# k transposed by DMA through bit planes from the ninth block on, its product with the decay on GpSimd, v loaded once

## The chip, the cores and the metric

One core of a Trainium2 chip runs the whole program. The metric is device microseconds of one execution, given as the median of the runs. The engines are called PE (matrix multiply), PEld (its weight loads), DVE (vector), ACT (scalar), POOL (GpSimd) and SP (here only a queue that issues DMAs).

## The reference

Three layers follow one another. The first is a linear attention with a state per head, the second a feed-forward layer with g = h·cos(h), the third a soft mixture of experts over all 3072 tokens.

```python
batch, n_heads, seq, head_dim = (4, 8, 768, 48)
for t in range(S):
    kt, vt, rt, wt = (k[:, :, t], v[:, :, t], r[:, :, t], w[:, :, t])
    cur = np.einsum('bhd,bhe->bhde', u[None] * kt, vt)
    y[:, :, t] = np.einsum('bhd,bhde->bhe', rt, state + cur)
    state = wt[:, :, :, None] * state + np.einsum('bhd,bhe->bhde', kt, vt)
...
h = x @ w_in
g = h * np.cos(h)
x = g @ w_out
...
logits = x @ phi                      # softmax over tokens fills slots, softmax over slots mixes them back
slot_out[e] = np.maximum(slot_input[e] @ w1[e], 0.0) @ w2[e]
```

All tensors are float32.

## The kernel before

The 3072 tokens go through in 24 blocks of 128 (six blocks per batch item; block j reads 128 steps of all eight heads). Blocks are numbered from 0. Inside a block the recurrence is cut into two chunks of 64 steps, c = 0 and 1.

For block j the attention steps are: `lw`, `lk`, `lr`, `lv`, `lz` load w, k, r, v (`lz` loads v a second time, with rows and heads placed so that it can stand beside the state in `rzs`, the stationary operand of the output). `wT`, `rT`, `kT` transpose w, r and k on PE, four 128x128 transposes each into one PSUM bank (`transpose4`, the call is line 145). `scan` and `sp` are two running products of the decay on DVE (L160 and L168). `ks` multiplies the transposed k with the decay on DVE (L195), `kN` transposes that back on PE (L213), `ksn` copies it to SBUF, `A` is the attention inside a chunk (L206), `U` the sum of k times v (L257). `z` (POOL from block 5 on, L267) decays the state, `st` adds U to it (DVE, L278), `rz` copies it into `rzs` (ACT), `y` is the output of the block (PE, L289). `ru`, `bo`, `bs` and `D` make the term with u: two products on POOL (L173, L174), a sum on DVE, two small copies on ACT, and a diagonal written by POOL (L220).

The feed-forward layer works on pieces h.t.q: block t, q one of four groups of 512 hidden columns. `h` is nine matmuls (L443 to L445), then `turns` (ACT), `rest` (DVE), `cos` (ACT), `mul` (DVE) make g. Of each block's four pieces three are transposed by DMA in blocks 3 to 19: `gz` copies the 32-bit values on ACT into two planes of 16 bits (L492), `gd` writes the planes to DRAM (L497), `gx` reads them back with a DMA transpose (L501). The rest is transposed on PE (`gT`) and copied (`gc`). `l` multiplies with phi folded into w_out (L510). `sum` to `es` are the running softmax over tokens. After the last block a fixed part computes the experts and the output (lines 722 to 891); the weights of the experts are loaded by `att`, `we` and `late0`.

The order of everything up to there is written out in the string `HEAD`: one word per step, and each engine, and the queue of SP, carries out its instructions in the order of that list. A DMA on SP waits in the queue for what it reads, and everything behind it waits with it. The first third of the list also decodes the weights of the feed-forward layer on ACT and DVE. The PSUM pool `ps_a` has three banks, which `wT`, `rT`, `kT`, `kN`, `A`, `U` and `y` take in turn.

Of the kernel before, what the change touches and what calls it, by code (L numbers as in the profile page):

```python
# [22 lines left out]
def rwkv_moe_kernel(ctx: ExitStack, tc: tile.TileContext, r, k, v, w, u, w_in, w_out, phi, w1, w2, cst, out):  # L23
    nc = tc.nc
# [255 lines left out]
    def e_y(j):  # L280

        L, rz = lt[j % 2], rzs[j % 2]
# [781 lines left out]
```

## Time and profile before

| | us |
|---|---|
| median of 3 runs | 482.76 (482.46 to 484.51) |
| the profiled execution, whole | 482.29 |
| its span | 480.5 |
| PE busy | 452.2 (94%) |
| DVE busy | 403.0 (84%) |
| ACT busy | 356.0 (74%) |
| POOL busy | 122.3 (25%) |

The span runs from the first to the last instruction of the trace; 1.8 us of the profiled execution lie around it. Matmuls overlap each other in the trace, so a busy PE says only that one was under way; the step from one start to the next is what it really takes.

### The profile page before, as it was taken

The numbers are of one execution on the slowest core, as the hardware profiler recorded it, in microseconds if no ns is written. First come the engines' busy times: TensorE is split into PE (matmuls) and PEld (weight loads), VectorE is DVE, ScalarE is ACT, GpSimd is POOL, SyncE is SP. The second block draws the span as 40 slices with busy tenths as digits, with TensorE's granted clock in tenths as the row PEclk, the third lists the DMA queues.
The fourth block names the chain that finished last, engine by engine and source line by source line (L and its number), as shares of the span: only waits on it lengthen the run. The fifth ranks groups of instructions, "written<-read, shape, count | busy, mean of one in ns | idle before, by whom it ended". The sixth has DMA issues, their size and how long they took to land.

```text
span 480.5 us, 15374 instructions
## 1 busy us (share of the span) xinstructions
PE 452.2 (94%) x6313; PEld 345.6 (72%) x6313; DVE 403.0 (84%) x783; ACT 356.0 (74%) x727; POOL 122.3 (25%) x162
## 2 busy tenths in 40 slices
PE   1889899999999999999999999999999999988993
PEld 1567688887877878767778678687787777755573
DVE  3999999998998999999999999899998986665242
ACT  5799989877788788877877787778888655573242
POOL 2421231423433223023325121513323000002110
PEclk9999999999999999999999999999999999999997
DMA  9998999343795984799679979977769879699938
GB/s 214 309 297 211 171 211 208 59 74 84 139 199 127 162 173 139 153 193 172 140 158 158 204 157 177 188 120 149 179 135 130 233 256 411 247 337 405 368 125 272
DMA packets 205589, 94.21 MB, mean 196 GB/s; under 512 B 181840, under 2 KB 187216, under 8 KB 205520
## 3 DMA queue, kind: packets, MB, share of 16 engines
q1 hardware_dynamic: 205520, 93.23, 81.1%
q8 instruction: 50, 0.82, 0.7%
q14 instruction: 19, 0.16, 0.1%
HBM read 61.75 MB, written 18.09 MB: 166 GB/s over the span
## 4 chain that ended last, share of the span: by engine, by line
PE 74%; DVE 11%; ACT 5%; DMA 4%; SPq 3%; issue 1%; POOL 0%; ACTq 0%; POOLq 0%
PE h L443 12%; PE h L445 11%; PE h L444 11%; PE l L510 5%; PE E L606 4%; PE y L289 4%; PE gT L478 4%; PE A L206 3%; PE U L257 3%; PE hps L797 2%; PE so L834 2%; PE wT L145 2%; PE kT L145 2%; DVE g L462 2%; PE rT L145 2%; PE kN L213 2%
## 5 line engine op out<-in xcount | busy, mean ns | idle before, releaser
L443 PE MATMUL h<-wu,x 128*128 128x512 f32 x288 | 121.9, 423 | 0.2
L445 PE MATMUL h<-wu,x 128*128 128x512 f32 x288 | 113.2, 393 | 0.0
L444 PE MATMUL h<-wu,x 128*128 128x512 f32 x288 | 112.6, 391 | 0.0
L466 ACT ACTIVATE g<-g,half_pi 128x512 f32<-128x512 f32 (+1 forms) x97 | 69.5, 720 | 17.0 <-DVE g L462 16.0
L458 ACT ACTIVATE g<-h 128x512 int32<-128x512 f32 (+1 forms) x96 | 57.1, 595 | 32.9 <-PE h L445 25.0
L471 DVE TENSOR_TENSOR g<-g,h 128x512 f32<-128x512 f32 x96 | 64.7, 676 | 9.0 <-ACT g L466 8.1
L462 DVE SCALAR_TENSOR_TENSOR g<-g,h 128x512 f32<-128x512 int32 (+1 forms) x96 | 64.7, 675 | 8.6 <-ACT g L458 7.7
L443 PEld LDWEIGHTS h<-wu,x 128*128 128x128 f32 x288 | 54.3, 189 | 18.2 <-DVE g L471 2.3
L445 PEld LDWEIGHTS h<-wu,x 128*128 128x128 f32 x288 | 54.0, 188 | 12.3
L444 PEld LDWEIGHTS h<-wu,x 128*128 128x128 f32 x288 | 54.4, 189 | 8.7
L220 POOL TENSOR_SCALAR_AFFINE_SELECT lt<-bo 64x512 f32<-64x512 f32 x48 | 38.0, 793 | 68.1 <-ACT bo L248 57.7
L492 ACT COPY zg<-g 128x1024 uint16<-128x1024 uint16 x51 | 52.8, 1042 | 1.8 <-DVE g L471 1.2
L267 POOL TENSOR_TENSOR z<-st_state,qt 128x192 f32<-128x192 f32 x35 | 22.0, 629 | 118.3 <-DVE st_state L278 94.2
L173 POOL TENSOR_TENSOR ru<-rn,u_b 128x384 f32<-128x384 f32 x24 | 26.1, 1086 | 81.5 <-DVE bo L243 32.1
L275 ACT COPY rzs<-z 64x192 f32<-64x192 f32 x96 | 33.4, 348 | 1.4 <-DVE z L263 0.4
L232 DVE COPY_PREDICATED lt<-cs,A 64x256 f32<-64x256 uint32 x72 | 32.2, 447 | 1.9 <-PE A L206 0.4
L189 DVE TENSOR_TENSOR lt<-rT,pt 64x512 f32<-64x512 f32 x48 | 32.8, 684 | 0.8 <-PE rT L145 0.3
L168 DVE TENSOR_TENSOR_SCAN pt<-wf,ini_f 128x520 f32<-128x520 f32 x24 | 30.9, 1289 | 0.0
L160 DVE TENSOR_TENSOR_SCAN qt<-wf,one_b 128x520 f32<-128x520 f32 x24 | 29.8, 1242 | 0.0
L289 PEld LDWEIGHTS y<-lt,rzs 128*32 128x32 f32 x1536 | 23.5, 110 | 6.2 <-issue 3.7
L174 POOL TENSOR_TENSOR ru<-ru,kn 128x384 f32<-128x384 f32 x24 | 26.9, 1120 | 2.0 <-DMA kn<-in_k_dram 0.2
L478 PE MATMUL gT<-cs,g 128*128 128x128 f32 x180 | 27.1, 275 | 0.0
(175 smaller groups left out, 808.7 us busy)
## 6 DMA issues: line engine op xcount, KB each, us to landing
we<-in_moe_w_dram SPq DMA_DIRECT2D x16, 1536.0 KB, 9.3
gs<-zg SPq DMA_DIRECT2D x51, 256.0 KB, 2.5
rawo<-in_moe_w_out_dram SPq DMA_DIRECT2D x8, 768.0 KB, 5.1
wn<-in_w_dram SPq DMA_DIRECT2D x24, 192.0 KB, 4.6
kn<-in_k_dram SPq DMA_DIRECT2D x24, 192.0 KB, 4.3
rn<-in_r_dram SPq DMA_DIRECT2D x24, 192.0 KB, 4.5
vn<-in_v_dram SPq DMA_DIRECT2D x24, 192.0 KB, 4.2
rzs<-in_v_dram SPq DMA_DIRECT2D x96, 48.0 KB, 3.1
```

The lines of the kernel that those rows point to most:

```text
L220: nc.gpsimd.affine_select(out=lt[j % 2][h, a], in_=bo_t[j][h, a].unsqueeze(2).to_broadcast([64, NS, C]), pattern=[[0, NS], [-1, C]], compa ...
L275: nc.scalar.copy(rzs[j % 2][64 * a:64 * a + 64, c, :, a, RZ[a]], z_t[j, c][64 * a:64 * a + 64])
L289: nc.tensor.matmul(ps[m:m + 32, o, c * C:(c + 1) * C], lhsT=rz[:, c, p, a, 32 * b:32 * b + 32], rhs=L[:, a, 2 * p + c, :], start=m not in ...
L443: nc.tensor.matmul(half[:, f], lhsT=xh[:, c, :], rhs=wh, start=(c == 0), stop=False)
L444: nc.tensor.matmul(half[:, f], lhsT=xl[:, c, :], rhs=wh, start=False, stop=False)
L445: nc.tensor.matmul(half[:, f], lhsT=xh[:, c, :], rhs=wl, start=False, stop=(c == KD - 1))
L458: nc.scalar.activation(gt.bitcast(I32), hp, AF.Copy, bias=0.25, scale=1.0 / TWO_PI)
L462: nc.vector.scalar_tensor_tensor(out=gt, in0=gt.bitcast(I32), scalar=-TWO_PI, in1=hp, op0=ALU.mult, op1=ALU.add)
L466: nc.scalar.activation(gt, gt, AF.Sin, bias=half_pi[:, 0:1])
L471: (nc.gpsimd if pool else nc.vector).tensor_tensor(out=gt, in0=gt, in1=hp, op=ALU.mult)
L478: nc.tensor.transpose(ps[:, m * 128:(m + 1) * 128], gt[:, m * 128:(m + 1) * 128], ident)
L492: copy(zg, g_t[t, q].bitcast(U16).rearrange("p (f i) -> p i f", i=2))
```

## The change

From block 8 on (`JK`) the step `kT` is gone. In its place `kz` copies the loaded k on POOL into two planes of 16 bits, `kd` writes them to DRAM and `kx` reads them back with a DMA transpose, in the manner and with the buffers of `gz`, `gd` and `gx` (which get one more `gx` buffer). `ks` then reads SBUF and not PSUM, and runs on POOL. `lv` is gone for all 24 blocks: `vc` copies on POOL half of what `U` needs from the tile that `lz` has loaded, and `U` reads the other half straight from there; `rzs` gets a third buffer. The tile `pts` moves to another pool. The list `HEAD` is a new one, with the same steps otherwise.

```diff
+    JK = range(8, 24)
+    NRZ = 3
-    NGS = 51
+    NGS = 67
-    NGX = 4
+    NGX = 5
-    vn = [nat.tile([128, H, D], F32, name=f"vn{i}") for i in range(2)]
+    vn = [nat.tile([128, HP, D], F32, name=f"vn{i}") for i in range(2)]
-    rzs = [nat.tile([128, 2, HP, 2, 64], F32, name=f"rzs{i}") for i in range(2)]
+    rzs = [nat.tile([128, 2, HP, 2, 64], F32, name=f"rzs{i}") for i in range(NRZ)]
+    def copy_v(j):
+        for c in range(2):
+            nc.gpsimd.tensor_copy(vn[j % 2][64 * c:64 * c + 64], rzs[j % NRZ][64 - 64 * c:128 - 64 * c, c, :, c, RZ[c]])
-        nc.vector.tensor_tensor(out=ks, in0=ps, in1=segs(qt, 2, C), op=ALU.mult)
+        (nc.gpsimd if j in JK else nc.vector).tensor_tensor(out=ks, in0=ps, in1=segs(qt, 2, C), op=ALU.mult)
-  ... rhs=vn[j % 2][h, 2 * p + a], start=True, stop=True)
+  ... rhs=vn[j % 2][h, p] if a == c else rzs[j % NRZ][h, c, p, a, RZ[a]], start=True, stop=True)
-        wt_t["p", u_] = aw.tile([128, 128], F32, tag="pts", name=f"pts{u_}", bufs=1)
+        wt_t["p", u_] = sm_p.tile([128, G], F32, tag="lg", name=f"pts{u_}", bufs=1)[:, 0:128]
+    def e_kz(j):
+        zg = xb_p[0].tile([128, 2, 512], U16, tag="zg", name=f"zk{j}", bufs=NZG)
+        nc.gpsimd.tensor_copy(zg, kn[j % 2].rearrange("p h d -> p (h d)").bitcast(U16).rearrange("p (f i) -> p i f", i=2))
+        zg_t["k", j] = zg
+    def e_kd(j):
+        b_gd("k", j)
+    def e_kx(j):
+        b_gx("k", j)
+        pend["kT", j] = gt_t.pop(("k", j))
...
-raw.i.1 raw.i.0 q.i.1 lw.0 abs.i.1 cs lk.0 q.i.0 lr.0 ... lv.0 rT.0 wf.0 d2b.i.0
```

What the new list does to the engines is shown at three places near the end of the attention. In the names a number is a running count of tiles; `kn_122` holds k of an odd block, `ks` the product, `gx` and `gxk` transposed pieces.

PE, before, from the transpose of k of block 23 (`kT`) to its `kN`, with the two pieces of h between them cut to their first row:

```order
L510 MATMUL l_6000<-gx_1_5975,p_sb 32x128 x4
L145 MATMUL kT_6013<-cs,kn_122 128x128 x4
L443 MATMUL h_1_6024<-wu_322,x_116 128x512
...
L145 MATMUL rT_6034<-cs,rn_120 128x128 x4
L443 MATMUL h_2_6041<-wu_468,x_116 128x512
...
L510 MATMUL l_6000<-gx_2_6039,p_sb 32x128 x4
L510 MATMUL l_6000<-gt_3_5927,p_sb 32x128 x4
L478 MATMUL gT_1_6075<-cs,g_1_6055 128x128 x4
L213 MATMUL kN_6082<-cs,ks_6020 128x128 x4
```

PE, in the changed kernel, the same place (`ks_6091` is the product of block 23, `gx_1_6042` the piece whose DMA stands just ahead of k's on SP):

```order
L450 MATMUL h_2_6070<-wu_482,x_116 128x512
L451 MATMUL h_2_6070<-wu_482,x_116 128x512
L528 MATMUL l_5980<-gx_1_6042,p_sb 32x128 x4
L151 MATMUL rT_6112<-cs,rn_120 128x128 x4
L484 MATMUL gT_0_6120<-cs,g_0_6049 128x128 x4
L219 MATMUL kN_6125<-cs,ks_6091 128x128 x4
L484 MATMUL gT_1_6130<-cs,g_1_6080 128x128 x4
```

The transpose of k is gone, and `kN` now follows a product that another engine makes from a DMA.

SP, in the changed kernel, the end of the queue of transposes (`gsk_5773` are the planes of k of block 23 in DRAM):

```order
L503 DMA gs_1_5977<-zg_1_5900 128x1024
L507 DMA_TRANSPOSE gx_1_6000<-gs_1_5883 128x4x256
L507 DMA_TRANSPOSE gx_2_6005<-gs_2_5916 128x4x256
L507 DMA_TRANSPOSE gx_1_6042<-gs_1_5977 128x4x256
L507 DMA_TRANSPOSE gxk_6085<-gsk_5773 128x4x256
L503 DMA gs_2_6094<-zg_2_5998 128x1024
L503 DMA gs_0_6101<-zg_0_6047 128x1024
```

k's transpose is the fourth in a row there; before, no DMA stood between the load of k and the use on PE.

POOL, before, from the second `z` of block 21 to the first of block 22:

```order
L267 TENSOR_TENSOR z_1_5603<-st_state,qt_5333 128x192
L173 TENSOR_TENSOR ru_5697<-rn_120,u_b 128x384
L174 TENSOR_TENSOR ru_5697<-ru_5697,kn_122 128x384
L267 TENSOR_TENSOR z_0_5822<-st_state,qt_5459 128x192
L267 TENSOR_TENSOR z_1_5880<-st_state,qt_5459 128x192
```

POOL, in the changed kernel, between the same two (`zk` are planes of k, `vn` the copies of v):

```order
L273 TENSOR_TENSOR z_1_5679<-st_state,qt_5339 128x192
L226 AFFINE_SELECT lt_128<-bo_5379 64x512 x2
L511 COPY zk_5739<-kn_122 128x1024
L143 COPY vn_126<-rzs_131 64x192 x2
L201 TENSOR_TENSOR ks_5843<-gxk_5733,qt_5551 128x512
L226 AFFINE_SELECT lt_127<-bo_5665 64x512 x2
L143 COPY vn_125<-rzs_130 64x192 x2
L273 TENSOR_TENSOR z_0_5922<-st_state,qt_5551 128x192
```

Where two instructions stood between the two steps of the state there are now ten.

## Rows read from the trace of the kernel before

**Rows 1.** The page: span, and busy time of the engines.

```profile
span 480.5 us, 15374 instructions
PE 452.2 (94%) x6313; PEld 345.6 (72%) x6313; DVE 403.0 (84%) x783; ACT 356.0 (74%) x727; POOL 122.3 (25%) x162
```

**Rows 2.** Busy us by stretch: PE, PEld, DVE, ACT, POOL; clock, DMA share, GB/s.

```profile
0.00:90.00 90.00, 74.77 (x963) 57.00 (x963) 78.79 (x116) 77.49 (x150) 27.21 (x43) 1.00 0.94 220
90.00:380.00 290.00, 288.33 (x4132) 223.92 (x4130) 269.14 (x537) 230.82 (x468) 87.92 (x108) 1.00 0.78 152
```

**Rows 3.** Waits of PE from 90 to 380 us: total, times, longest.

```profile
PE U L257 <- DVE lt L189: 0.5, 1, 0.5
PE E L606 <- DVE ltok L593: 0.3, 1, 0.3
PE E L606 <- ACT dt L587: 0.2, 1, 0.2
```

**Rows 4.** Timeline of PE around two transposes: start us, length us, what.

```profile
341.37 0.66 PE L145 MATMUL kT<-cs,kn 128*128 128x128 f32 x4
341.78 0.48 PE L443 MATMUL h<-wu,x 128*128 128x512 f32 x1
342.10 0.39 PE L444 MATMUL h<-wu,x 128*128 128x512 f32 x1
342.33 0.40 PE L445 MATMUL h<-wu,x 128*128 128x512 f32 x1
...
343.95 0.60 PE L145 MATMUL rT<-cs,rn 128*128 128x128 f32 x4
344.30 0.48 PE L443 MATMUL h<-wu,x 128*128 128x512 f32 x1
```

**Rows 5.** Single lines and tiles: ns least/median/most, first and last start.

```profile
L195 DVE TENSOR_TENSOR ks<-kT,qt x24: 642/683/692, 13.1 to 377.9; 128x512 f32<-128x512 f32 x24
...
L168 DVE TENSOR_TENSOR_SCAN pt<-wf,ini_f x24: 1224/1234/1808, 13.6 to 370.9; 128x520 f32<-128x520 f32 x24
...
L173 POOL TENSOR_TENSOR ru<-rn,u_b x24: 992/1010/1954, 14.0 to 355.3; 128x384 f32<-128x384 f32 x24
...
L220 POOL TENSOR_SCALAR_AFFINE_SELECT lt<-bo x48: 651/656/1567, 20.7 to 369.2; 64x512 f32<-64x512 f32 x48
...
L267 POOL TENSOR_TENSOR z<-st_state,qt x35: 509/516/1457, 93.0 to 385.7; 128x192 f32<-128x192 f32 x35
```

**Rows 6.** The page's groups: busy us, mean ns, idle before them.

```profile
L220 POOL TENSOR_SCALAR_AFFINE_SELECT lt<-bo 64x512 f32<-64x512 f32 x48 | 38.0, 793 | 68.1 <-ACT bo L248 57.7
L267 POOL TENSOR_TENSOR z<-st_state,qt 128x192 f32<-128x192 f32 x35 | 22.0, 629 | 118.3 <-DVE st_state L278 94.2
```

**Rows 7.** Timeline of POOL and DVE around one scan.

```profile
146.47 1.00 POOL L173 TENSOR_TENSOR ru<-rn,u_b 128x384 f32<-128x384 f32 x1
146.76 1.81 DVE L168 TENSOR_TENSOR_SCAN pt<-wf,ini_f 128x520 f32<-128x520 f32 x1
...
147.55 1.83 POOL L174 TENSOR_TENSOR ru<-ru,kn 128x384 f32<-128x384 f32 x1
```

**Rows 8.** DMA issues: count, KB each, median us to landing.

```profile
gs<-zg SPq DMA_DIRECT2D x51, 256.0 KB, 2.5
...
vn<-in_v_dram SPq DMA_DIRECT2D x24, 192.0 KB, 4.2
...
gx<-gs SPq DMA_TRANSPOSE x51, 3.9
```

**Rows 9.** Time of one issue on SP's queue, ns least/median/most, first and last start.

```profile
L497 SPq DMA_DIRECT2D gs<-zg x51: 332/378/1772, 116.1 to 375.7; - x51
L501 SPq DMA_TRANSPOSE gx<-gs x51: 1226/1299/2444, 122.6 to 378.5; - x51
```

**Rows 10.** Timeline of PE: the matmuls on the last transposed pieces.

```profile
382.98 0.86 PE L510 MATMUL l<-gx,p_sb 128*32 128x128 f32 x24
```

**Rows 11.** Waits of the first 90 us.

```profile
ACT qi L346 <- DMA rawi<-in_moe_w_in_dram: 4.6, 3, 3.6
```

More of the change, by code (lines that the diff above doesn't have):

```diff
@@ L132, in load_rz @@
         b, t0 = bt(j)
-        rz = rzs[j % 2]
+        rz = rzs[j % NRZ]
         for c in range(2):
@@ L256, in e_U @@
                     h = slice(64 * c, 64 * c + 64)
-                    nc.tensor.matmul(ps[c][64 * a:64 * a + 64, p], lhsT=ksn[h, p * 128 + 64 * a:p * 128 + 64 * a + 64], rhs=vn[j % 2][h, 2 * p + a], start=True, stop=True)
+                    nc.tensor.matmul(ps[c][64 * a:64 * a + 64, p], lhsT=ksn[h, p * 128 + 64 * a:p * 128 + 64 * a + 64], rhs=vn[j % 2][h, p] if a == c else rzs[j % NRZ][h, c, p, a, RZ[a]], start=True, stop=True)
         pend["U", j] = ps
@@ L280, in e_y @@
     def e_y(j):
[L282 removed]
+        L, rz = lt[j % 2], rzs[j % NRZ]
         ps = tps(f"y{j}")[:, 0:DM].rearrange("p (c t) -> p c t", c=KD)
@@ new lines @@
+gz.4.1 rT.8 st.7.0 D.8 z.7.1 rest.4.2 kd.10 gz.4.0 kd.9 gT.2.3 h.5.0 gx.3.2 gx.3.1 kx.9 es.0 l.3.1 lr.10 l.3.2 l.2.2 gd.4.0 l.3.3 st.7.1 lr.9 gc.2.3
+L.8 cos.4.2 turns.5.0 mul.4.2 l.2.3 A.8 rz.7.1 kN.8 rest.5.0 sum.1 z.8.0 scan.9 h.4.3 lc.1 cos.5.0 mul.5.0 rz.7.0 ru.10 lw.10 mask.8 gd.4.1 ksn.8 ks.9
+gz.4.2 turns.4.3 sr.9 max.1 exp.1 rest.4.3 gx.4.0 xt.1 xr.1 lz.9 gz.5.0 h.5.1 xd.1 U.8 vc.9 cos.4.3 st.8.0 z.8.1 gd.4.2 kN.9 gx.4.1 dT.1 ltok.1
+mul.4.3 l.4.0 dc.1 y.7 lw.11 ksn.9 E.1.0 rz.8.1 xh.7 turns.5.1 sp.9 bo.10 wT.10 xl.7 h.5.2 wf.10 U.9 lk.12 gx.4.2 E.1.1 kx.10 l.4.1 rest.5.1 st.8.1
@@ new lines @@
+gd.5.0 rz.8.0 ru.9 cos.5.1 rT.9 z.9.0 turns.5.2 scan.10 mul.5.1 rest.5.2 h.6.1 lz.10 gz.5.1 cos.5.2 gd.5.1 bo.9 kz.12 sr.10 L.9 mul.5.2 rz.9.0 lk.11
+st.9.0 bs.9 turns.6.1 sp.10 y.8 gx.5.0 z.9.1 gz.5.2 D.9 rest.6.1 xh.8 l.4.2 gd.5.2 cos.6.1 h.5.3 xl.8 gT.4.3 wT.11 turns.5.3 mul.6.1 st.9.1 rest.5.3
+rT.10 gc.4.3 gx.5.1 lr.12 wf.11 cos.5.3 h.6.3 L.10 mul.5.3 A.9 scan.11 gT.5.3 bs.10 rz.9.1 kz.11 ks.10 h.6.0 z.12.0 turns.6.3 gx.5.2 gz.6.1 kN.10
+l.5.0 kd.11 rest.6.3 lw.12 l.5.1 l.5.2 z.10.0 cos.6.3 vc.10 mask.9 gc.5.3 es.1 l.5.3 turns.6.0 lz.11 ksn.10 mul.6.3 l.4.3 U.10 sum.2 kd.12 lr.11
@@ new lines @@
+ru.20 mul.15.0 rest.15.2 cos.15.2 z.19.0 wf.20 gz.15.0 h.15.3 wT.21 mul.15.2 ks.19 mask.18 h.16.1 y.17 lw.22 gx.14.2 l.14.1 gd.15.0 turns.15.3 bs.19
+rest.15.3 l.14.2 gz.15.2 rT.19 cos.15.3 scan.20 mul.15.3 turns.16.1 xh.17 gT.15.3 gd.15.2 h.16.3 rest.16.1 sr.20 rz.18.0 gx.15.1 cos.16.1 xl.17
+gx.15.0 turns.16.3 D.19 gx.15.2 kN.19 lr.21 ksn.19 gc.15.3 es.6 mul.16.1 gz.16.1 L.19 vc.19 kd.20 rest.16.3 kx.20 h.16.0 U.19 l.15.0 cos.16.3 sp.20
+l.14.3 l.15.1 st.19.0 l.15.2 wf.21 bo.20 kz.21 z.19.1 turns.16.0 mul.16.3 l.15.3 sum.7 A.19 rest.16.0 cos.16.0 cmb.0.5 lc.7 max.7 mul.16.0 exp.7
@@ new lines @@
+rest.17.2 sp.21 h.18.0 cos.17.2 wf.22 lr.22 A.20 ks.21 mul.17.2 gx.17.0 gz.17.2 turns.18.0 gT.17.3 gd.17.1 gx.16.2 h.19.1 L.21 gc.17.3 kN.21 scan.22
+bs.21 rest.18.0 cos.18.0 l.16.1 vc.21 mask.20 l.16.2 l.17.0 gd.17.2 l.16.3 mul.18.0 ksn.21 U.21 gz.18.0 ru.22 rz.20.1 sr.22 h.18.1 gx.17.1 l.17.1 y.20
+turns.19.1 gx.17.2 es.7 bo.22 l.17.2 l.17.3 kd.22 lk.23 st.21.0 z.21.1 sp.22 gd.18.0 turns.18.1 rest.19.1 cos.19.1 sum.8 st.21.1 lz.23 rest.18.1
+mul.19.1 D.21 A.21 rz.21.1 cos.18.1 lc.8 mask.21 xh.20 max.8 kx.22 lz.22 kz.23 exp.8 mul.18.1 h.19.2 rT.22 cmb.1.5 turns.19.2 rest.19.2 xt.8 kd.23
```

175 lines of the change are left out of this document (80 added, 95 removed).

## The prediction, made before the changed kernel ran

> **What bounds the kernel now.** I read the busy times by engine first. PE is busy for 452.2 of 480.5 us [rows 1], but matmuls overlap in the trace, so I went on to the stretches. From 90 to 380 us, the stage in which all blocks from 8 on have their k transposed, PE is busy for 288.3 of 290 us, DVE for 269.1, ACT for 230.8 and POOL for 87.9 [rows 2]. The reader is to see there that PE has no room, DVE 20.9 us, and POOL more than two thirds of the stage. The granted clock is 1.00 throughout, so it plays no part. Then the waits of PE in that stage: three, 1.0 us together [rows 3]. PE carries out one list, in order, and almost never stands still, so what comes out of PE's list in this stage comes out of the time, as long as no new wait comes in. The first 90 us are different: DVE and ACT, busy for 78.8 and 77.5 us, decode weights and PE has only 74.8 us of work [rows 2].
>
> **The transposes removed.** Blocks 8 to 23 lose `kT`, 16 times four transposes. The timeline prints 0.66 us for one such group, but that includes overlap. What PE really pays is the step from the group's start to the next start, 341.37 to 341.78 = 0.41 us, and then the first matmul of h behind it takes 0.32 us to the next one where the following takes 0.23: 0.09 more [rows 4]. That is 0.50 us, and 16 x 0.50 = 8.0 us. Bounds: the neighbouring group for r steps in 0.35 us, 0.44 with the same 0.09 [rows 4], so 7.0 us; the printed 0.66 us gives 10.6. I take 8.0, because it is read at a `kT` itself.
>
> **DVE.** It loses 16 `ks` of 0.683 us [rows 5] = 10.9 us and would be busy for 258 us of a stage of about 282: still behind PE. This gives nothing on top, but it means that the engine next in line does not take over the bound.
>
> **POOL.** The changed `ks` is 128x512 with two inputs. POOL's products take 1.010 us for 384 columns and 0.516 us for 192 [rows 5], 2.57 ns a column, so 512 columns are about 1.34 us. `kz` reads 1024 values of 16 bits, one input. No such operation of POOL is in the trace. The nearest is the diagonal, one input, 512 columns in 0.656 us [rows 5], which doubled is 1.31 us; by the column price of two inputs it would be 2.63 us. I take 1.35, with both ends kept. `vc` is two copies of 64x192; by the diagonal's price 0.25 us each, by that of `z` 0.52. I take 0.5 us for the pair, at most 1.03. A block then adds 1.34 + 1.35 + 0.5 = 3.2 us, at most 5.0. POOL's means lie above its medians (0.793 against 0.656 us for the diagonal, 0.629 against 0.516 for `z` [rows 5, 6]), a fifth more, so I count 3.8 us, at most 6.0. Over 16 blocks that is 61 us, at most 96, on top of 87.9: POOL would be busy for 149 to 184 us of 282. It is not the bound by sum. What it can do is come late, which is a rival below.
>
> **DMA and SP.** Each `kd` moves 256 KB and lands after 2.5 us, each `kx` after 3.9 us [rows 8]. Two hand-overs and `ks` included, k takes some 6.4 + 1.35 + 1.34 = 9.1 us from `kz` to `kN` where it took one transpose and 0.68 us of DVE. A block lasts about 16 us (24 `ks` from 13.1 to 377.9 us [rows 5]), so the list has room to start it a block ahead. SP's queue is charged 0.38 + 1.30 us per block [rows 9], 26.8 us in all, and gives up 24 issues of v. The bytes added, 16 x 512 KB = 8.4 MB, stand against 24 x 192 KB = 4.7 MB removed [rows 8]. The DMA share in the stage is 0.78 [rows 2] and no wait of PE there names a DMA [rows 3]. So: nothing on the path if the list is kept; if that cover goes, PE waits at `kN`.
>
> How tight can it be? The last transposed piece of before is issued at 378.5 us [rows 9], lands about 3.9 us later [rows 8], at 382.4, and the matmuls on it start at 382.98 [rows 10] without any wait of PE in a row. So the mechanism was run with 0.6 us to spare and held. But k has one station more, `ks` on POOL. In the changed order of block 23, `kx` stands right behind the piece `gx_1_6042`, and on PE only one transpose of r and one of g lie between the use of that piece and `kN`, about 1 us, while `kx` is issued one issue (1.30 us) later and needs 1.34 us more. So I expect a wait of some 1 to 2 us at places like this one. I charge +1.0 us for new waits in all, which doubles the 1.0 us that the stage has now. The bounds are 0 and 8, half a microsecond per block.
>
> **v, `rzs`, `pts`.** `U` reads the same values at the same shapes from other places, and `rzs` waits for the block three back and not two. Price 0, hidden behind PE's list. In the first 90 us the DMA share is 0.94 [rows 2], and there the five or so loads of v that fall away are 1 MB, at 220 GB/s 4.5 us of transfers. ACT waits for the weights' DMA for 4.6 us there [rows 11]. But `lz` must now land before `U`, which it did not have to, and the decoding is held by DVE and ACT themselves. I take 0, with bounds of -4.5 and, half of that the other way, +2.
>
> **Sum.** 480.5 - 8.0 + 1.0 = 473.5 us of span, and with the 1.8 us around it 475.3 us. The profiled execution was 482.3, the median of the runs 482.8, so 0.5 us lies between them; I leave the forecast at 475.3.
>
> **A rule that speaks against it.** The scan at 146.76 us starts while POOL's product of 146.47 is still running and takes 1.81 us; POOL's next product, behind it, takes 1.83 us and ends after the scan [rows 7]. Alone that product takes 1.01 [rows 5]. So each engine holds the other up for about the rest of its instruction. The Trainium skill (SBUF — State Buffer, section "SBUF: two separate sides") says why: DVE instructions with two SBUF inputs and GpSimd instructions take a shared pair of ports as an exclusive lock, and the loser is blocked for the whole instruction. The trace agrees for the scans. What this costs DVE today is small: of the 24 scans of L168 half take at most 1.234 us, next to the least of 1.224, and the worst 1.808 [rows 5]. With POOL busy for half of the stage and not 30% more of them will meet it, but 0.57 us apiece for a few more fits into DVE's idle time. That is why it is a rival and no term.
>
> **The rivals.**
> *The lock makes DVE the bound.* If each of the 32 scans of blocks 8 to 23 is held up by 0.57 us, the worst less the median (1.808 - 1.234 [rows 5]), DVE has 18.4 us more and stands at 258 + 18.4 = 276 of 282. If half of its present idle time of 20.9 us can't be given up, the stage is 276 + 10.5 = 286.5 us, 3.5 less than now: 478.8 us. Against it: at 30% of POOL only a few scans show any of it.
> *POOL comes late and the state with it* (the other side). At the place that I showed, ten instructions stand between two `z` where two stood, some 6.5 us of work. Now POOL idles 94.2 us for the state before `z` [rows 6], so `z` always goes at once. If `ks` waits for a late `kx`, all that stands behind it waits: `z`, then `st`, `rz`, `y`, and then h of the next block on PE. It decides from 0.50 us of PE waits per block (8.0 / 16). At 1.0 us per block: 480.5 - 8 + 16 + 1.8 = 490 us. For it: `kz` may cost 2.63 us and not 1.35. Against it: the idle time is large, and 6.5 us fit into a block of 16.
> *The transposes go but waits of PE eat most of it.* 4 us of waits at `kN` in all, two or so at each place like block 23's: 480.5 - 8 + 4 + 1.8 = 478.3; with 7 us 481.3, which is no change.
> *The start gains too.* With the 4.5 us of transfers gone and PE never waiting anew: 480.5 - 8 - 4.5 + 1.8 = 469.8 us.
>
> **How the numbers follow.** The forecast with its own bounds (472 to 477.5): 0.48. The start gains, under 472: 0.12. Waits eat some, 477.5 to 480.3: 0.16; eat all, about 481 to 485: 0.08. The lock, around 479: 0.06, half of it within no change. POOL late, over 485: 0.10. A measurement of this kernel can tell about 0.5%, 2.4 us, from no change: 480.35 to 485.2. Faster: 0.48 + 0.12 + 0.16 + 0.03 = 0.79; same 0.11; slower 0.10. The range from 470.5 to 481.5 leaves out about 0.05 below and 0.15 above.
>
> **What would show it.** PE has no transposes of k from 110 us on, 64 fewer matmuls, and the stage is some 7 us shorter with PE's waits still at 1 to 3 us: right. `ks` on POOL at 1.2 to 1.6 us and `kz` at 1.3 to 2.6: right. Wrong would be rows of waits of PE at `kN` for POOL, or at `y` and h behind a late `z`, more than 8 us together; scans with a median near 1.8 us; or a start that is longer than 90 us for the same work.

## The result and the profile after

The changed kernel takes 486.29 us (median of 20 runs, 483.73 to 490.3), the kernel before 482.87 us beside it (20 runs). The ratio is 1.0068, with a 95% interval of 1.005 to 1.0085: 0.7% slower, where 475.3 us had been forecast. The profiled execution took 483.81 us, one of the shortest of its kernel, so its trace shows 1.5 us of a loss that is 3.4 us at the median.

The page of the changed kernel, to be held against [rows 1]:

```profile
span 482.1 us, 15370 instructions
PE 446.9 (93%) x6249; PEld 336.2 (70%) x6249; DVE 400.5 (83%) x767; ACT 355.3 (74%) x727; POOL 179.5 (37%) x244
```

64 matmuls and 5.3 us of PE's busy time are gone, and the span is 1.6 us longer. What the span has beside PE's busy time, PE's idle time, grew from 28.3 to 35.2 us. So of the 8.6 us between the span forecast (473.5) and the one measured, 5.9 are idle time (6.9 more, where 1.0 was charged), and 2.7 are busy time that should have gone (8.0) and did not (5.3). DVE has lost 16 `ks` of 0.683 us [rows 5], 10.9 us, but is busy only 2.5 us less. The stretches of [rows 2]:

```profile
0.00:90.00 90.00, 73.67 (x956) 56.55 (x957) 79.24 (x114) 76.92 (x150) 33.24 (x54) 1.00 0.86 209
90.00:380.00 290.00, 282.48 (x4058) 213.99 (x4057) 266.74 (x528) 227.82 (x460) 137.28 (x177) 1.00 0.86 168
```

PE now stands still for 7.5 of 290 us where it was 1.7, and the DMA share is 0.86 instead of 0.78. The waits of PE in that stage (total, times, longest) were three, 1.0 us together [rows 3]; now they are:

```profile
PE h L449 <- DVE g L477: 1.4, 4, 0.5
PE wT L151 <- DVE st_state L284: 1.3, 1, 1.3
PE l L528 <- DMA gx<-gs: 1.0, 2, 0.7
PE y L295 <- DVE lt L238: 0.8, 1, 0.8
PE E L624 <- DVE ltok L611: 0.7, 1, 0.7
PE wT L151 <- PE gT L484: 0.6, 1, 0.6
PE dT L598 <- ACT g L472: 0.5, 1, 0.5
PE E L624 <- ACT dt L605: 0.3, 1, 0.3
PE y L295 <- ACT bo L254: 0.2, 1, 0.2
```

They are small, have many names, and none is `kN`. The 2.7 us of busy time stand in no row of waits; they are read from the steps. From the last matmul of a piece of h to the next start it is 0.32 us when `A` follows and 0.23 when `kN` does, here in the changed kernel:

```profile
343.88 0.39 PE L451 MATMUL h<-wu,x 128*128 128x512 f32 x1
344.20 0.70 PE L212 MATMUL A<-lt,ks 64*64 64x64 f32 x32
...
347.15 0.39 PE L451 MATMUL h<-wu,x 128*128 128x512 f32 x1
347.38 0.60 PE L219 MATMUL kN<-cs,ks 128*128 128x128 f32 x4
```

Ahead of `A`, `U`, `y`, `l` and `E` this step is 0.32 to 0.34 us on average. Added up over the trace there are 14 such places in the kernel before, 22 with the same edits under the old order (e2 below) and 53 in the changed kernel, about 0.1 us more each time; waits left out, h steps through 3.9 us more in all. The last 16 groups of `kT` in the kernel before step through 7.5 us together. So the transposes were worth about what was forecast, and the new order gave a part of it back.

To see where the time lies I use one measure throughout: the first and the last start of the first matmul line of h, which cut the program into a start, a middle that holds all 16 transposes removed, and an end. Single lines, the kernel before and then the changed one:

```profile
L443 PE MATMUL h<-wu,x x288: 276/397/590, 32.2 to 423.7; 128*128 128x512 f32 x142, 128*128 128x256 f32 x2
```

```profile
L449 PE MATMUL h<-wu,x x288: 280/397/591, 34.3 to 425.3; 128*128 128x512 f32 x143, 128*128 128x256 f32 x1
```

The start grew by 2.1 us, and the middle went from 391.5 to 391.0. The cut is not quite the same in both: the new list has `A` of block 1 ahead of the first h and the old one behind it, 32 matmuls that step through 1.0 us. So about 1.1 us of the start are a loss, and by the prediction's terms (-8.0 + 1.0) the middle should be 384.5, or 383.5 without that `A`: 7.5 us were lost there. The end is the same, 56.8 us after the last h in both.

The new work of POOL and its neighbours in the changed kernel (ns least/median/most):

```profile
L201 POOL TENSOR_TENSOR ks<-gxk,qt x16: 1187/1197/1785, 128.8 to 378.2; 128x512 f32<-128x512 f32 x16
...
L511 POOL COPY zk<-kn x16: 1035/1036/1253, 108.4 to 355.2; 128x1024 uint16<-128x1024 uint16 x16
...
L143 POOL COPY vn<-rzs x48: 339/342/1602, 16.9 to 364.9; 64x192 f32<-64x192 f32 x48
...
L166 DVE TENSOR_TENSOR_SCAN qt<-wf,one_b x24: 1224/1235/1652, 11.5 to 364.6; 128x520 f32<-128x520 f32 x24
...
L174 DVE TENSOR_TENSOR_SCAN pt<-wf,ini_f x24: 1221/1233/2055, 13.0 to 368.5; 128x520 f32<-128x520 f32 x24
...
L273 POOL TENSOR_TENSOR z<-st_state,qt x35: 506/516/1509, 93.7 to 388.7; 128x192 f32<-128x192 f32 x35
```

`ks` and `kz` cost less than forecast, the copies of v a little more, and the scans' medians did not move; in all the 48 scans took 1.6 us more. Where a wait comes from is seen in the chain that ended last, at its longest detour from PE (start us, us, what):

```profile
243.07 0.10 PE h L450
243.17 3.69 DMA rn<-in_r_dram
...
247.00 1.01 POOL ru L179
...
248.09 1.02 POOL ru L180
...
249.17 1.17 POOL vn L143
...
250.40 0.34 POOL vn L143
...
250.81 0.66 POOL lt L226
...
251.53 0.65 POOL lt L226
252.19 0.49 POOL z L273
...
252.70 0.36 DVE st_state L284
253.06 0.59 DVE g L468
```

A load of r goes out late on SP. `ru` at the head of POOL's queue waits for it, the copies of v, the diagonal and `z` stand behind `ru`, DVE waits 1.7 us for `z`, and the `wT` of the list above waits for the bank that `st` frees. From there to 270 us the chain stays on DVE. SP's queue had changed too. What it waited for from ACT between 90 and 425 us, before and after:

```profile
SPq L497 <- ACT zg L492: 46.7, 26, 4.1
```

```profile
SPq L503 <- ACT zg L498: 15.2, 13, 2.1
```

The queue waits for its data a third as long as it did.

### The profile page after: what moved, and what is told of

Same layout as the page of the kernel before. It is cut to its first block, busy times and chain, and to the rows that moved or that the text cites. A ratio compares the mean times of both kernels' runs of the same rounds, so it can differ in the third digit from the quotient of the medians.

```text
span 482.1 us, 15370 instructions
## 1 busy us (share of the span) xinstructions
PE 446.9 (93%) x6249; PEld 336.2 (70%) x6249; DVE 400.5 (83%) x767; ACT 355.3 (74%) x727; POOL 179.5 (37%) x244
## 4 chain that ended last, share of the span: by engine, by line
PE 57%; DVE 18%; ACT 8%; DMA 8%; issue 3%; SPq 3%; POOL 2%; ACTq 0%; DVEq 0%; POOLq 0%
PE h L449 9%; PE h L451 8%; PE h L450 8%; PE E L624 4%; PE gT L484 3%; PE y L295 3%; PE l L528 3%; DVE g L468 2%; DVE g L477 2%; PE hps L815 2%; PE so L852 2%; PE A L212 2%; DVE lt L238 2%; DMA gs<-zg 2%; DMA gx<-gs 2%
## 5 line engine op out<-in xcount | busy, mean ns | idle before, releaser
L449 PE MATMUL h<-wu,x 128*128 128x512 f32 (+1 forms) x288 | 121.9, 423 | 1.5 <-DVE g L477 1.4
L451 PE MATMUL h<-wu,x 128*128 128x512 f32 (+1 forms) x288 | 113.2, 393 | 0.0
L450 PE MATMUL h<-wu,x 128*128 128x512 f32 (+1 forms) x288 | 112.6, 391 | 0.0
L464 ACT ACTIVATE g<-h 128x512 int32<-128x512 f32 x96 | 57.1, 595 | 27.1 <-PE h L451 21.6
L468 DVE SCALAR_TENSOR_TENSOR g<-g,h 128x512 f32<-128x512 int32 x96 | 64.6, 674 | 11.0 <-ACT g L464 9.9
L477 DVE TENSOR_TENSOR g<-g,h 128x512 f32<-128x512 f32 (+1 forms) x96 | 64.9, 676 | 8.0 <-ACT g L472 6.6
L273 POOL TENSOR_TENSOR z<-st_state,qt 128x192 f32<-128x192 f32 x35 | 23.5, 672 | 65.6 <-DVE st_state L284 25.5
L226 POOL TENSOR_SCALAR_AFFINE_SELECT lt<-bo 64x512 f32<-64x512 f32 x48 | 35.0, 728 | 24.6 <-ACT bo L254 14.6
L143 POOL COPY vn<-rzs 64x192 f32<-64x192 f32 x48 | 21.4, 447 | 45.1 <-DMA rzs<-in_v_dram 39.4
L238 DVE COPY_PREDICATED lt<-cs,A 64x256 f32<-64x256 uint32 x72 | 32.3, 448 | 2.9 <-PE A L212 0.8
L166 DVE TENSOR_TENSOR_SCAN qt<-wf,one_b 128x520 f32<-128x520 f32 x24 | 31.2, 1299 | 0.3 <-ACT wf L161 0.2
L201 POOL TENSOR_TENSOR ks<-gxk,qt 128x512 f32<-128x512 f32 x16 | 20.5, 1281 | 28.8 <-PE A L212 16.2
```

The costliest lines, as they stand in the source:

```text
L226: nc.gpsimd.affine_select(out=lt[j % 2][h, a], in_=bo_t[j][h, a].unsqueeze(2).to_broadcast([64, NS, C]), pattern=[[0, NS], [-1, C]], compa ...
L238: nc.vector.copy_predicated(out=lt[j % 2][h, a, c::2], mask=mask[h].bitcast(U32).unsqueeze(1).to_broadcast([64, HP, C]), data=ps[a][o, 0:HP])
L449: nc.tensor.matmul(half[:, f], lhsT=xh[:, c, :], rhs=wh, start=(c == 0), stop=False)
L450: nc.tensor.matmul(half[:, f], lhsT=xl[:, c, :], rhs=wh, start=False, stop=False)
L451: nc.tensor.matmul(half[:, f], lhsT=xh[:, c, :], rhs=wl, start=False, stop=(c == KD - 1))
L464: nc.scalar.activation(gt.bitcast(I32), hp, AF.Copy, bias=0.25, scale=1.0 / TWO_PI)
```

## The experiments

Each kernel was timed beside the kernel before on the same chip. "First to last h" is from each run's profile; a run is read against 391.5 us (before) or 391.0 (changed); the lists of e1, e2 and e17 have `A` of block 1 where the old one has it, the others of the changed kernel where the new one has it. e5, e7, e8, e11 and e12 leave work out and are no versions to use. A number "behind its list" in an expectation is the time of an h less the sum of PE's steps listed ahead of it.

| run | us | ratio to before (95%) | first to last h |
|---|---|---|---|
| changed kernel | 486.3 | 1.0068 (1.005 to 1.0085) | 34.3 to 425.3 = 391.0 |
| e1_old_list_v | 492.8 | 1.0201 (1.0174 to 1.0228) | 35.9 to 431.3 = 395.4 |
| e2_old_list_vk | 505.9 | 1.0492 (1.0447 to 1.0537) | 35.8 to 443.4 = 407.6 |
| e3_ks_on_dve | 495.4 | 1.0249 (1.022 to 1.0278) | 34.6 to 434.5 = 399.9 |
| e4_v_halves_by_dma | 497.9 | 1.03 (1.0263 to 1.0337) | 36.6 to 441.3 = 404.7 |
| e5_no_k_transfers | 483.8 | 1.0008 (0.9989 to 1.0027) | 36.4 to 424.8 = 388.4 |
| e6_small_issues | 500.7 | 1.0347 (1.0318 to 1.0375) | 34.1 to 441.9 = 407.8 |
| e7_after_half_L | 484.5 | 1.001 (0.9987 to 1.0032) | 36.5 to 424.4 = 387.9 |
| e8_before_half_L | 482.4 | 0.9975 (0.9954 to 0.9997) | 32.9 to 423.0 = 390.1 |
| e9_before_small_issues | 491.9 | 1.0175 (1.0147 to 1.0203) | 32.9 to 431.9 = 399.0 |
| e10_before_gpsimd_work | 488.0 | 1.01 (1.0073 to 1.0127) | 32.4 to 429.5 = 397.1 |
| e11_after_all_relieved | 479.6 | 0.9932 (0.991 to 0.9953) | 36.1 to 421.2 = 385.1 |
| e12_after_gpsimd_relief | 483.5 | 1.0013 (0.9991 to 1.0035) | 36.2 to 424.7 = 388.5 |
| e13_start_load | 485.9 | 1.0059 (1.004 to 1.0078) | 36.4 to 427.5 = 391.1 |
| e14_v_from_act_queue | 509.2 | 1.0543 (1.0512 to 1.0575) | 36.7 to 451.8 = 415.1 |
| e15_before_v_from_act | 509.7 | 1.0556 (1.0528 to 1.0583) | 32.3 to 449.4 = 417.1 |
| e16_v_copies_on_act | 491.4 | 1.0184 (1.0153 to 1.0214) | 37.2 to 433.1 = 395.9 |
| e17_old_list_v_from_6 | 488.9 | 1.0127 (1.0096 to 1.0157) | 32.2 to 428.4 = 396.2 |
| e18_new_list_v_from_6 | 495.5 | 1.0254 (1.0217 to 1.0291) | 35.2 to 436.8 = 401.6 |

### Parts of the change under the old and the new order

e1, the code of the changed kernel with the old list, where in each block j `lv` is dropped, `vc` put just ahead of `U`, and `lz` moved ahead of that where it came later (for block 0 to the head of the whole list, ahead of the weights and of `cs`):

```diff
-lv.j
+vc.j
-    JK = range(8, 24)
+    JK = ()
```

> Old list, kT still on TensorE, ks still on VectorE; only v is loaded once (two GpSimd copies per block put 2.5 us of TensorE time ahead of U). Three theories for why the change came out 3.4 us slower (486.3 against 482.9) though TensorE lost 7.5 us of transposes. List theory: the new order places VectorE's and ScalarE's work so late that TensorE waits, whatever the edits. POOL theory: GpSimd's in-order queue (z, ks, vc, kz) makes z and through it the state late. DMA theory: the 33 further transfers per side for k make gx late and uneven. Here, list theory: 482 to 483 (old order, no edit on TensorE). POOL theory: the 21 us of v copies cost part, 483 to 485. DMA theory: fewer DMA descriptors (v once), 481 to 482.5.

Measured 492.8: 10 us slower with v loaded once and its loads and copies put in by hand. Of its trace 3.7 us lie ahead of the first h, 3.9 between the first and the last, and 1.3 behind. No theory had that.

e2, the same with all the edits, from block 8 on:

```diff
-kT.j
+kz.j kd.j kx.j
```

> Old list with all the edits: from block 8 on kT is taken out, kz, kd and kx are put in 15.5, 13 and 9 us of TensorE time ahead of ks, ks on GpSimd, v loaded once. List theory: the 7.5 us saved stay, 475 to 478, and the edits are good. POOL theory: no better than the new list, 484 to 488. DMA theory: 484 to 488 too, with l waiting for gx. Caution: without kT the three PSUM banks of that pool rotate otherwise than the old order was made for, which may cost 1 to 3 us by itself.

Measured 505.9, far above all three: put into the old order by hand the edits cost 23 us, in the new order 3.4. So the edits are dearer in the old order than in the new one; what the new order costs without the edits was not run. How much of the 23 us is the other rotation of the banks, or the places chosen by hand, the run does not tell.

e3:

```diff
-        (nc.gpsimd if j in JK else nc.vector).tensor_tensor(out=ks, ...
+        nc.vector.tensor_tensor(out=ks, ...
```

> The changed kernel, its list as it is, only ks of blocks 8 to 23 back on VectorE (reads the transposed k from SBUF). GpSimd loses 20.5 us, VectorE gains 16 times about 0.68 us = 10.9 us. POOL theory: faster by 1 to 4 us (482 to 485). List theory: VectorE is the late engine, so its added 10.9 us show on TensorE: 489 to 494. DMA theory: no change, 486.

Measured 495.4, 9.1 us more than the changed kernel for 10.9 us of work on DVE, as the list theory had it. DVE, 83% busy, has little room to spare in this order.

e4:

```diff
-            nc.gpsimd.tensor_copy(vn[j % 2][64 * c:64 * c + 64], rzs[...])
+            nc.sync.dma_start(vn[j % 2][64 * c:64 * c + 64], v[b, :, t0 + c * C:t0 + (c + 1) * C, :]...[c])
```

> The changed kernel, only the two GpSimd copies of v per block replaced by two loads of the same halves from memory, asked for 9 us of TensorE time ahead of U. GpSimd loses 21.4 us of copies and their 39 us of waits for rzs at the head of its queue; DMA gains 48 loads, 2.4 MB. POOL theory: faster by 1 to 4 us, 482 to 485. List theory: within 1 us of 486.3. DMA theory: slower by 1 to 3 us, 487 to 489.

The list puts `vc` earlier, as the expectation says. Measured 497.9, 11.6 more. What GpSimd saved went unnoticed beside 48 more loads. Too much for 2.4 MB, which is why a fourth theory came in: the queue that hands transfers out.

### One resource at a time

e5:

```diff
     def e_kd(j):
-        b_gd("k", j)
+        zg_t.pop(("k", j))
     def e_kx(j):
-        b_gx("k", j)
-        pend["kT", j] = gt_t.pop(("k", j))
+        pend["kT", j] = one_b[:, 0:512]
```

> The changed kernel and its list, without the two transfers of k per block (16 writes gsk, 16 transposing reads gxk); kz is still made, ks multiplies the decay by ones instead of k (so the recurrence of blocks 8 to 23 has no k). SyncE's queue loses 36.7 us of issuing between 90 and 425 us (26.6 gxk, 10.1 gsk) of 262.5; GpSimd, VectorE and the order stay. A fourth theory joins: the queue theory, that SyncE's queue of transfers, 93% occupied from 125 to 350 us, hands out rn, rzs, gs and gx late, GpSimd's queue head then waits for them, and z, the state, VectorE and at last TensorE are late. Queue theory and DMA theory: 475 to 479. List theory (VectorE's order): 484 to 487. POOL theory: 484 to 487, since GpSimd has the same work.

Measured 483.8: 2.5 us less than the changed kernel, not 7 to 11. The transfers of k are a part, not the whole.

e6:

```diff
     def e_kx(j):
         ...
+        for i in range(2):
+            nc.sync.dma_start(gs_p.tile([1, 16], F32, ...), cst[0:1, 0:16])
```

> The changed kernel with two further transfers of 64 bytes each put on SyncE's queue behind every gxk of blocks 8 to 23: 32 issues, 2 KB in all, read by nobody. Queue theory: at about 0.5 us of issuing each, 16 us more in the queue, 2 to 6 us slower: 488 to 492. DMA theory (bytes and engines): no change, 486 to 487. List and POOL theory: no change.

Measured 500.7, 14.4 us more, for 2 KB. The row of these issues on SP's queue (ns least/median/most), and the first of PE's waits from 90 to 380 us:

```profile
L521 SPq DMA_DIRECT2D tiny<-in_const_dram x32: 568/582/1355, 113.3 to 391.1; - x32
```

```profile
PE l L530 <- DMA gx<-gs: 5.8, 7, 1.8
PE h L449 <- DVE g L477: 2.8, 4, 1.3
```

32 x 0.582 = 18.6 us of issuing cost 14.4 us of time. So it is the place in the queue and not the bytes; the DMA theory falls, and the queue theory has its limit shown. But with e5 it is a limit from one side only: more costs most of it, less gives little.

e7 and e8, the same edit in the changed kernel and in the one before:

```diff
-        for a in range(2):
+        for a in range(2 if j < 8 else 1):
             h = slice(64 * a, 64 * a + 64)
             nc.vector.tensor_tensor(out=L[h, a], in0=ps[h], in1=segs(pt, 0, C)[h], op=ALU.mult)
```

> The changed kernel with one of the two VectorE multiplications of L left out in blocks 8 to 23 (that half of lt is stale): VectorE loses 16 times 0.68 = 10.9 us evenly over the middle, as much as ks on VectorE added in the run before (which cost 9.1 us). List theory (VectorE late): 476 to 480. Queue, DMA and POOL theory: VectorE waits longer instead, 484 to 486.

> The kernel before with the same half of L left out in blocks 8 to 23, 10.9 us less on VectorE. If TensorE alone bounds it there, as the prediction held: 480 to 482.5, only its small waits go. If VectorE's order holds TensorE back in it as in the changed kernel: 474 to 478. What is left between this run and the one with the changed kernel is what the edits give when VectorE has slack: -7 us if the 7.5 us of transposes are then gained.

Measured 484.5 and 482.4: 1.8 us less in the changed kernel, 0.4 in the one before. DVE behaves like the queue: 10.9 us more cost 9.1, 10.9 less give 1.8.

### The kernel before under the same loads

e9:

```diff
     def e_kT(j):
         pend["kT", j] = transpose4(kn[j % 2], f"kT{j}")
+        if j >= 8:
+            for i in range(2):
+                nc.sync.dma_start(gs_p.tile([1, 16], F32, ...), cst[0:1, 0:16])
```

> The kernel before with the same 32 transfers of 64 bytes on SyncE's queue, two behind every kT of blocks 8 to 23. In the changed kernel they cost 14.4 us. If the queue was already at its limit before (247.6 us of issuing between 90 and 425): 490 to 497. If it had slack (it waited 46.7 us for ACT's zg there, against 15.2 in the changed kernel) and the change used that up: 483 to 487. The second is what the prediction took for granted when it hid the queue.

Measured 491.9, 9.1 more than before. From 90 to 380 us no row of PE's waits in the kernel before named a DMA [rows 3], and still half of the 32 x 0.584 = 18.7 us of issuing showed in the time. In the changed kernel it was three quarters (14.4 of 18.6): the queue had some room, and the change used up a part of it. The 46.7 us of waits for `zg` fell to 18.4 here, so they were slack only in part.

e10:

```diff
     def e_kT(j):
+            nc.gpsimd.tensor_copy(scr.bitcast(U16)..., kn[j % 2]...)
     def e_ks(j):
+            nc.gpsimd.tensor_tensor(out=scr..., in0=one_b..., in1=segs(qt, 2, C), op=ALU.mult)
     def e_U(j):
+            for c in range(2):
+                nc.gpsimd.tensor_copy(scr[64 * c:64 * c + 64, 0:192]..., vn[j % 2][64 * c:64 * c + 64, c::2])
```

> The kernel before with GpSimd work of blocks 8 to 23 like that of the change, whose results nobody reads: a copy of k as kz (about 1.04 us), a product as ks (1.2 us), two quarter copies of v (0.34 us each), 47 us in all, at the places of kT, ks and U. POOL theory, with z behind this work and VectorE's small operations held up beside it: 485 to 490, with VectorE's scans and small operations longer. If GpSimd's slack (25% busy) hides it: 482.5 to 484.

Measured 488.0, 5.2 more, as the POOL theory had it. The busy times of this run:

```profile
PE 455.0 (94%) x6313; PEld 346.4 (71%) x6313; DVE 408.6 (84%) x783; ACT 356.1 (73%) x727; POOL 168.8 (35%) x226
```

POOL has 46.5 us more than in [rows 1], and DVE, which was given nothing, is busy for 5.6 us more. Counted through the traces, every instruction of DVE that took over 0.1 us more than the shortest of its line and shape ran beside one of POOL: 11 of them in the kernel before, 5.5 us more together, 20 here with 11.1 us, and 28 in the changed kernel with 11.4 us. That is what the lock of the prediction's rival would do, which the Trainium skill has (SBUF — State Buffer, section "SBUF: two separate sides"). The trace agrees in the times. How much of the 5.2 us is DVE held up, and how much a later `z`, this run does not tell apart.

e12, and e11 with e5, e7 and e12 together:

```diff
-        nc.gpsimd.tensor_copy(zg, kn...)
+        nc.gpsimd.tensor_copy(zg[:, :, 0:32], kn...[:, :, 0:32])
-            nc.gpsimd.tensor_copy(vn[...], rzs[...])
+            d = slice(0, D if j < 8 else 4)
+            nc.gpsimd.tensor_copy(vn[...][:, :, d], rzs[...][:, :, d])
```

> The changed kernel with kz and the two copies of v cut to a sixteenth and a twelfth of their columns in blocks 8 to 23 (the writes of k take a tile of ones as source, same bytes): GpSimd loses some 28 us, VectorE, the transfers and the order stay. POOL theory: 480 to 483, scans and small VectorE operations back to the lengths of before. List and queue theory: 485 to 487.

> The changed kernel with three reliefs at once: no transfers of k (ks multiplies by ones), half of L left out in blocks 8 to 23, and kz and the copies of v cut to a sixteenth and a twelfth of their columns in blocks 8 to 23 (some 28 us less GpSimd work). If the loss is a sum of small waits on several engines that are all at their limit, the reliefs add up and the 7.5 us of transposes show: 474 to 479. If the order itself holds TensorE back, by the length of its chains from engine to engine: 480 to 484, hardly better than the single reliefs (483.8 and 484.5).

e12 measured 483.5, 2.8 less than the changed kernel, with 17.8 us less of POOL (161.7 against 179.5) where some 28 were expected. DVE is as busy in it as in the changed kernel, 400.9 against 400.5 us, so it is not by DVE's busy time that this relief helps. e11 measured 479.6, 6.7 less. The single reliefs add up to 2.5 + 1.8 + 2.8 = 7.1. The row of e11:

```profile
L450 PE MATMUL h<-wu,x x288: 280/395/591, 36.1 to 421.2; 128*128 128x512 f32 x143, 128*128 128x256 f32 x1
```

From the first to the last h it takes 385.1 us, where the prediction's terms gave 383.5 for this cut. So 5.9 of the 7.5 us lost in the middle come back. (Half of L is work that both kernels have, and without it the middle of e8 was 1.4 us shorter, so about that much is not the change's.) PE stands still for 3.6 us from 90 to 380 us, against 7.5 in the changed kernel and 1.7 before. So most of the loss in the middle is a sum of small waits on SP's queue, on POOL and on DVE. What stays is mainly the longer steps of the new order: PE is busy for 446.2 us in e11, 6.0 less than before and not 8.0.

### Moving work, and the start

e13, SP's order at the start:

```diff
-... lk.0 misc q.i.0 raw.i.3 d2b.i.1 d2a.i.0 lw.1 abs.i.0 wT.0 lz.0
+... lk.0 lw.1 misc q.i.0 raw.i.3 d2b.i.1 d2a.i.0 abs.i.0 wT.0 lz.0
```

> The changed kernel with one step of the list moved: the load of w of block 1 is asked for ahead of the two small constants, the third piece of the weights and the loads of v, as before the change. In the changed kernel TensorE stands idle for it from 14.8 to 16.5 us; in the profiles of four of its variants the granted clock then fell to 0.63 to 0.67 between 16 and 20 us and the first h came at 22.4 to 22.8 us behind its list instead of 20.6 (before: 19.2 to 19.8). If that is how 2 to 3 us of the loss arise: 483 to 484.5. If the start is made up for later: 486.

The expectation rests on the second `wT`, here in the timeline of the changed kernel and of e5:

```profile
16.54 0.63 PE L151 MATMUL wT<-cs,wn 128*128 128x128 f32 x4 [1.74 <-DMA wn<-in_w_dram]
```

```profile
16.80 0.80 PE L151 MATMUL wT<-cs,wn 128*128 128x128 f32 x4 [2.34 <-DMA wn<-in_w_dram]
```

and on the stretch behind it in the two (the granted clock is third from the end):

```profile
16.00:24.00 8.00, 6.53 (x87) 4.78 (x87) 7.63 (x11) 7.65 (x15) 4.25 (x4) 1.00 1.12 312
```

```profile
16.00:24.00 8.00, 6.12 (x53) 4.58 (x53) 6.52 (x10) 6.66 (x14) 4.00 (x5) 0.79 1.14 309
```

The two have the same order there. In the changed kernel the clock stayed at 2.4 GHz; in e5, behind the longer wait, the mean of 0.79 says that a part of the stretch ran at 1.2 GHz, and the first h came at 36.4 instead of 34.3. e13 measured 485.9, no gain to speak of: the clock held at 1.00 and the first h still came at 36.4. The load of w is early now and the third piece of weights late; ACT waits 8.0 us for the weights where it waited 6.5. One load put ahead in the queue puts another behind; whether that is all of it the run does not show.

e14 and e15, from block 6 on, in the kernel of e13 and in the one before:

```diff
-                nc.sync.dma_start(rz[...], vv[a])
+                (nc.scalar if j >= 6 else nc.sync).dma_start(rz[...], vv[a])
```

> The kernel of the run above, and the four loads of v of each block from 6 on put on ScalarE's queue instead of SyncE's: SyncE loses 66 of 262 us of issuing between 90 and 425 us, no byte is spared. Queue theory: 478 to 482 if an issue costs ScalarE little. If it costs ScalarE as much as SyncE (0.8 us each), ScalarE's 355 us become 410 and it is slower, 488 to 500. If only bytes and DMA engines matter: as the run above.

> The kernel before with the same four loads of v per block, from block 6 on, on ScalarE's queue. Its queue had 247.6 us of issuing between 90 and 425 us, and 32 small issues more cost it 9.1 us. If the queue holds it back as it is: 479 to 481.5. If it only just has room: 482 to 484; if an issue is dear on ScalarE: 485 to 495.

Measured 509.2 and 509.7. The loads' row on ACT's queue in e14:

```profile
L139 ACTq DMA_DIRECT2D rzs<-in_v_dram x72: 602/627/2021, 85.5 to 383.0; - x72
```

72 x 0.627 = 45 us of ACT, at a price of 23 us, 27 in the kernel before. An issue occupies ACT for as long as it does SP (0.614 us for the same row in the changed kernel). That the loads also come later, out of a queue in which they stand behind ACT's other work, may be part of the price: POOL's copies of v waited 51.9 us for them in e14 and 39.4 in the changed kernel. The Trainium skill (DMA: Bandwidth & Descriptors, section "Issuing engines are not separate DMA queues") says that issuing from several engines saves only the issuing time, usually small beside the transfer itself. Small it is here too, 0.627 us against 3.5 us to landing, and still 72 of them were not free.

e16:

```diff
-            nc.gpsimd.tensor_copy(vn[...], rzs[...])
+            (nc.gpsimd.tensor_copy if j < 8 else nc.scalar.copy)(vn[...], rzs[...])
```

> The kernel with the earlier start load, and the two copies of v per block from block 8 on made by ScalarE instead of GpSimd: GpSimd loses 14 us and what its queue waits for rzs, ScalarE gains 32 times about 0.35 us = 11 us. POOL theory with slack on ScalarE: 481 to 483. If ScalarE is at its limit like VectorE and the queue: 486 to 492.

Measured 491.4, 5.5 more than e13 for 11 us on ACT. ACT, 74% busy, passes on half of it.

e17 under the old order, e18 under the new one (blocks 0 to 5 load v into a tile that is free until then):

```diff
-                    ... rhs=vn[j % 2][h, p] if a == c else rzs[...]
+                    ... rhs=vf[j % 2][h, 2 * p + a] if j < 6 else vn[j % 2][h, p] if a == c else rzs[...]
```

> Old list, kT on TensorE and ks on VectorE, v loaded once from block 6 on only: blocks 0 to 5 load v twice as before the change, so that the start is that of the kernel before. With v loaded once in all blocks the old list took 492.8 us, its first h 3.7 us later than before. If the start's loss is due to the four loads of v that U of the first blocks then waits for, where one did: the first h as before (19 to 20 us behind the list) and 488 to 490; what is left over 482.8 is then the price of v in the middle with an order not made for it. If the start's loss comes from elsewhere: 492.

> The changed kernel with v loaded twice in blocks 0 to 5, one load where four stood ahead of U, the four only ahead of y; from block 6 on as changed. If the four loads ahead of the first U are the start's loss of some 3 us: 483 to 484.5, about the time before. If the new order of the start is slow for itself (as the run with the earlier load of w suggests, which kept its first h at 22.8): 486.

e17 measured 488.9, and its first h:

```profile
L450 PE MATMUL h<-wu,x x288: 276/395/587, 32.2 to 428.4; 128*128 128x512 f32 x142, 128*128 128x256 f32 x2
```

That is where the kernel before has it, 32.2; with v loaded once in all blocks (e1) it was 35.9. The time is as expected (488 to 490), the reason is not: most of the 3.7 us between them is no wait of `U` for v. 3.2 us of it are there at the first matmul, in the kernel before and in e1:

```profile
9.79 1.09 PE L145 MATMUL wT<-cs,wn 128*128 128x128 f32 x4 [9.79 <-DMA cs<-in_const_dram]
```

```profile
12.95 1.09 PE L151 MATMUL wT<-cs,wn 128*128 128x128 f32 x4 [12.95 <-DMA cs<-in_const_dram]
```

e1 has the four loads of v of block 0 at the head of its list, and their issues hold SP for 2.72 us before anything else goes out; `U` itself waits 0.9 us for the copies. So e1's start comes from that place. In the changed kernel these loads stand behind those of the weights, of w and of `cs`, and its start is not explained by e1. The middle still takes 4.7 us more than before: the copies and the earlier `lz`, in an order not made for them. e18 measured 495.5: its first h came at 35.2, but behind it, from 34 to 100 us, SP's loads wait 16.6 us for `U`, and PE waits 3.9 us in one place for k. So it says nothing on the new order's start.

## Why the prediction was wrong

**The transposes, -8.0 us: right for what was removed, too much for what was gained.** The 64 matmuls are gone, and the groups step through 7.5 us in the kernel before. But PE's busy time fell by 5.3 us. The sum took the new list for the old one without `kT`, and the new list has h next to other steps, which costs 3.9 us in steps that no row calls a wait.

**New waits, +1.0 us: the step that failed.** PE's idle time grew by 6.9 us: some 1.2 ahead of the first h, 5.7 in the middle, inside the bound of 8 but nearly six times the term. The named waits of PE from 90 to 380 us grew by 5.8 (6.8 against 1.0). And the mechanism was wrong: I expected them at `kN`, behind `kx`, and none is there. PE waits for DVE in most of them, at h, `wT`, `y` and `E`. POOL's `ks` waited 16.2 us for `A` to free its one buffer, and 1.4 are put down to k's transfer (and 5.3, in one place, to a load of r that it does not read).

**"DMA and SP: nothing on the path if the list is kept": wrong.** I read from PE's waits that the queue had room. e9 shows that the kernel before passed on half of what was added to it, and e5 prices the transfers of k at 2.5 us.

**POOL, priced at 0: wrong.** Its sum came out lower than forecast, 137 us in the stage and not 149 to 184; but a queue that is in order costs by what stands behind what, as the chain at 243 us shows. Relief gave 2.8 us (e12), the same kind of load in the kernel before cost 5.2 (e10).

**DVE, "gives nothing on top": half right.** It was to fall by 10.9 us and fell by 2.5. Part of the rest is POOL holding it up: e10 shows 5.6 us for 46.5 us of POOL, and the changed kernel has 28 lengthened instructions of DVE for 11. It is not mainly at the scans, as the rival had it: their medians stayed at 1.23 us, and all 48 took 1.6 us more. Small operations grew as well. One of them, `dl` in the softmax (ns least/median/most), before and after:

```profile
L532 DVE TENSOR_TENSOR dl<-mx,dl x11: 159/159/748, 137.6 to 432.5; 128x1 f32<-128x1 f32 x11
```

```profile
L550 DVE TENSOR_TENSOR dl<-mx,dl x11: 158/304/900, 141.4 to 434.1; 128x1 f32<-128x1 f32 x11
```

**The start, 0 with +2 as bound: wrong.** Seven profiles have the start of the changed list. In three (the changed kernel, e3, e6) the first h comes at 34.1 to 34.6 us and the granted clock stayed at 1.00; in four (e5, e7, e11, e12) it comes at 36.1 to 36.5, and from 16 to 20 us the clock is 0.63 to 0.67. One microsecond of either is the `A` that was moved. What causes the rest stays open: e13 and e18 did not bring it back, and e13 had its first h at 36.4 with the clock at 1.00. That the median lies 2.5 us above the profiled execution fits a start at about 36 us in most runs (e13, with a middle of 391.1, took 486.1); no trace of such a run of the changed kernel shows it.

**The rivals.** "Waits eat most of it" was the nearest: 7 us of waits were to give 481.3. The profiled execution has 6.9 us of them, though not at `kN`, and lies 2.5 us above that, since PE's list is 2.7 us longer than the terms had it. "POOL late" named a real chain (the one at 243 us) but priced it as if it came in every block. "The lock" is there, but did not make DVE the bound by its scans. The three reliefs were worth 2.5, 1.8 and 2.8 us; no one cause decides.

## What to carry to other kernels

When TensorE hardly waits in a kernel ordered by hand, that says nothing about room elsewhere: here the transfer queue, VectorE and ScalarE each passed on about half or more of what was added to them, and GpSimd a tenth. The queue and VectorE gave back far less when relieved. Before calling an edit hidden, add its load alone to the old kernel (32 empty transfers, a product that nobody reads) and time that: e9 and e10 would have told it in two runs. Count transfers by their number as well as by their bytes, and look at every in-order queue for what then stands behind the new step. When a list is ordered anew, add up TensorE's steps from start to start again: what stands next to what changes them without a wait.

## What the runs showed of the hardware that was not expected

A transfer of 64 bytes occupies the queue that issues it for 0.58 us, about as long as one of 48 KB (0.614 us in the changed kernel's `rzs`), and one of 48 KB from ScalarE's queue 0.63 us. 46.5 us of GpSimd work whose results nobody reads made VectorE busy for 5.6 us more, and a 128x1 operation of 0.16 us took up to 0.9 in the changed kernel (0.75 before). The step from the last matmul of h to the next start was 0.23 us ahead of transposes and 0.32 to 0.34 ahead of `A`, `U`, `y`, `l` and `E`. And with one and the same order at the start the granted clock of 16 to 24 us was 1.00 in one profile and 0.79 in another, with the first h 2.1 us apart. A start with waits in it may so spread the times of a kernel; no run here tests it.
